# Retention attention and a hard-swish feed-forward layer: from whole sequences to 128-position chunks, with DMA transposes and a Strassen down product

## The chip, the cores and the metric

The kernel runs on one core of a Trainium2 chip. The metric is the device time of one execution in microseconds. A kernel is timed several times and beside runs of the kernel before on the same chip. A product is summed in PSUM, TensorE's output memory; an eviction reads it from there, computes on it and writes the result to SBUF, the memory that matmuls read. The span is the time from the first to the last instruction of a run. In the profiles PE is TensorE (matmul), PEld its weight loads, DVE is VectorE, ACT is ScalarE, POOL is GpSimd, and SP is the engine whose queue issues most DMAs.

## The reference, cut to what matters

```python
batch, n_heads, seq, head_dim = (8, 8, 576, 64)     # q, k, v: float32
scores = (1 / 8) * q @ k.T                          # per batch and head
gamma  = 1 - 2 ** (-5 - h)                          # one decay per head
ret    = scores * where(i >= j, gamma ** (i - j), 0)
x      = (ret @ v) -> [8 * 576, 512]                # heads side by side
h = x @ w_in                                        # 512 -> 2048
g = h * clip(h + 3, 0, 6) / 6
out = g @ w_out                                     # 2048 -> 512, float32
```

There is no softmax: the decay is a power of the distance. So the part of a row that lies in earlier chunks can be carried as a 64 x 64 state per head.

Of the kernel before, what the change touches and what calls it, by code (L numbers as in the profile page):

```python
# [10 lines left out]
FP32 = mybir.dt.float32  # L12
# [6 lines left out]
def kernel(  # L19
# [9 lines left out]
    nc = tc.nc  # L29
    B, H, S, D = q.shape  # L30
# [3 lines left out]

    NCH = (S + P - 1) // P
    msz = [min(P, S - P * i) for i in range(NCH)]
    m1sub = []
    for tcix in range(NCH):
        lo = P * tcix
        subs = []  # L40
        while lo < S:
            hi = min(lo + 512, S)
            subs.append((lo, hi))
            lo = hi
        m1sub.append(subs)
    atoff = []
    o = 0
    for tcix in range(NCH):
        atoff.append(o)
        o += S - P * tcix  # L50
    ATW = o
    m2sc = [(0, 288), (288, 576)]

    gamma = [1.0 - 2.0 ** (-5.0 - h) for h in range(H)]
    NFULL = S // P
    REM = S - NFULL * P

    const = ctx.enter_context(tc.tile_pool(name="const", bufs=1))
    work = ctx.enter_context(tc.tile_pool(name="work", bufs=3))
    big = ctx.enter_context(tc.tile_pool(name="big", bufs=1))  # L60

    ident16 = const.tile([P, P], FP16)
    make_identity(nc, ident16)
    cb = const.tile([P, 2], FP32)
    nc.gpsimd.memset(cb[:, 0:1], 0.5)
    nc.gpsimd.memset(cb[:, 1:2], float(np.log(0.125)))

    rsel = const.tile([P, ATW], FP32)
    for tcix in range(NCH):
        W = S - P * tcix  # L70
        nc.gpsimd.iota(rsel[:, atoff[tcix]:atoff[tcix] + W],
                       pattern=[[1, W]], base=0, channel_multiplier=-1,
                       allow_small_or_imprecise_dtypes=True)
        nc.gpsimd.affine_select(
            out=rsel[:, atoff[tcix]:atoff[tcix] + W],
            in_=rsel[:, atoff[tcix]:atoff[tcix] + W], compare_op=ALU.is_ge,
            fill=1.0e8, base=0, pattern=[[1, W]], channel_multiplier=-1)
    dmask = const.tile([P, H, ATW], FP16)
    for h in range(H):
        nc.scalar.activation(dmask[:, h, :], rsel, ACTF.Exp,  # L80
                             bias=cb[:, 1:2], scale=float(np.log(gamma[h])))

    win16 = big.tile([P, DM // P, DFF], FP16)
    wout16 = big.tile([P, DFF // P, DM], FP16)

    NCC = DM // P
    xt16 = big.tile([P, NCC, NTOK], FP16)

    psum = ctx.enter_context(tc.tile_pool(name="psum", bufs=8, space=bass.MemoryType.PSUM))

    def cast_load(src4, b, h, dst, coloff, width):
        last = (b == B - 1 and h == H - 1)
        if not last:
            fl = src4[b, h].rearrange("s d -> (s d)")
            ap = bass.AP(tensor=fl.tensor, offset=fl.offset,
                         ap=[[D, P], [P * D, NCH], [1, D]])
            nc.gpsimd.dma_start(dst[:, :, coloff:coloff + D], ap)
        else:
            nc.gpsimd.dma_start(
                dst[:, 0:NFULL, coloff:coloff + D],  # L100
                src4[b, h, 0:NFULL * P, :].rearrange("(j p) d -> p j d", p=P))
            nc.gpsimd.dma_start(dst[0:REM, NFULL, coloff:coloff + D],
                                src4[b, h, NFULL * P:S, :])
            nc.gpsimd.memset(dst[REM:P, NFULL, coloff:coloff + D], 0.0)

    NFC = DFF // P
    MBLK = 512
    NMB = NTOK // MBLK
    chunkq = []
    moe_state = {}  # L110

    def moe_unit(kb, kind, ix):
        tok0 = kb * MBLK
        if kind == 0:
            if ix == 0:
                moe_state[kb] = work.tile([P, NFC, MBLK], FP16, tag="gt16",
                                          bufs=2, name=f"gt16_{kb}")
            gt16 = moe_state[kb]
            fc = ix
            ph = psum.tile([P, MBLK], FP32, tag="pp")  # L120
            for dmc in range(NCC):
                nc.tensor.matmul(ph, win16[:, dmc, P * fc:P * fc + P],  # L122
                                 xt16[:, dmc, tok0:tok0 + MBLK],
                                 start=(dmc == 0), stop=(dmc == NCC - 1))
            u = work.tile([P, MBLK], FP32, tag="moeu", bufs=4)
            nc.scalar.activation(u, ph, ACTF.Relu, bias=cb[:, 0:1],  # L126
                                 scale=1.0 / 6.0)
            nc.vector.scalar_tensor_tensor(out=gt16[:, fc, :], in0=u,  # L128
                                           scalar=1.0, in1=ph,
                                           op0=ALU.min, op1=ALU.mult)  # L130
        else:
            gt16 = moe_state[kb]
            mc = ix
            pout = psum.tile([P, DM], FP32, tag="pp")
            for fc in range(NFC):
                nc.tensor.matmul(pout, gt16[:, fc, P * mc:P * mc + P],  # L136
                                 wout16[:, fc, :],
                                 start=(fc == 0), stop=(fc == NFC - 1))
            osb = work.tile([P, DM], FP32, tag="osb", bufs=4)
            nc.scalar.copy(osb, pout)  # L140
            nc.sync.dma_start(out[tok0 + P * mc:tok0 + P * mc + P, :], osb)

    def pop_units(n):
        for _ in range(n):
            if chunkq:
                moe_unit(*chunkq.pop(0))

    bready = [((kk + 1) * MBLK - 1) // S for kk in range(NMB)]
    xbar_i = [0]

    for b in range(B):
        if b > 0:
            for kk in range(NMB):
                if bready[kk] == b - 1:
                    for fc in range(NFC):
                        chunkq.append((kk, 0, fc))
                    for mc in range(MBLK // P):
                        chunkq.append((kk, 1, mc))
            pop_units(4)
        for c in range(H // 2):  # L160
            pop_units(1)
            qn16 = work.tile([P, NCH, 2 * D], FP16, tag="nat16", bufs=18)
            kn16 = work.tile([P, NCH, 2 * D], FP16, tag="nat16", bufs=18)
            vn16 = work.tile([P, NCH, 2 * D], FP16, tag="nat16", bufs=18)
            for h2 in range(2):
                cast_load(q, b, 2 * c + h2, qn16, h2 * D, D)
                cast_load(k, b, 2 * c + h2, kn16, h2 * D, D)
                cast_load(v, b, 2 * c + h2, vn16, h2 * D, D)
            qtk2 = []
            for nix, nat in enumerate((qn16, kn16)):  # L170
                pst = psum.tile([P, S], FP16, tag="pp")
                for j in range(NCH):
                    sj = msz[j]
                    nc.tensor.transpose(pst[:, P * j:P * j + sj],  # L174
                                        nat[0:sj, j, :], ident16[0:sj, 0:sj])
                sb = work.tile([P, S], FP16, tag="qtk", bufs=10)
                if nix == 0:
                    nc.vector.tensor_copy(sb, pst)  # L178
                else:
                    nc.scalar.copy(sb, pst)  # L180
                qtk2.append(sb)
            qt2, kt2 = qtk2
            pop_units(2)
            at16a = work.tile([P, ATW], FP16, tag="at16", bufs=6)
            at16b = work.tile([P, ATW], FP16, tag="at16", bufs=6)
            at16s = [at16a, at16b]
            bgrp = [[(0, 0, 512, 0)],
                    [(0, 512, S, 0), (1, P, S, 64)],
                    [(2, 2 * P, S, 0), (3, 3 * P, S, 320)],
                    [(4, 4 * P, S, 0)]]  # L190
            for grp in bgrp:
                pm0 = psum.tile([P, 512], FP32, tag="pp")
                pm1 = psum.tile([P, 512], FP32, tag="pp")
                pms = [pm0, pm1]
                for (tcix, a, bb, co) in grp:
                    mt = msz[tcix]
                    ns = bb - a
                    for h2 in range(2):
                        base = h2 * D
                        nc.tensor.matmul(pms[h2][0:mt, co:co + ns],  # L200
                                         kt2[base:base + D,
                                             P * tcix:P * tcix + mt],
                                         qt2[base:base + D, a:bb],
                                         start=True, stop=True)
# [11 lines left out]
            for (s0, s1) in m2sc:  # L216
# [4 lines left out]
                for tcix in range(NCH):  # L221
                    lo = max(s0, P * tcix)
                    if lo < s1:
                        contrib.append((tcix, lo))
# [32 lines left out]
    while chunkq:  # L257
        moe_unit(*chunkq.pop(0))
# [30 lines left out]
```

## The kernel before: what the change and the argument touch

All matmuls are fp16. For each batch and pair of heads it loads and casts q, k and v by DMA, transposes q and k on TensorE, computes all scores on and above the block diagonal (1600 columns per head), multiplies them by a stored decay table on VectorE, and multiplies by v. Units of the feed-forward product (up: 512-wide, down: 512-wide) are popped between these steps.

```python
for b in range(B):
    ...
    for c in range(H // 2):                          # a pair of heads
        pop_units(1)
        ...                                          # loads, 10 transposes, 2 copies
        pop_units(2)
        bgrp = [[(0, 0, 512, 0)], [(0, 512, S, 0), (1, P, S, 64)],
                [(2, 2 * P, S, 0), (3, 3 * P, S, 320)], [(4, 4 * P, S, 0)]]
        for grp in bgrp:
            ...                                      # scores into pm0, pm1 (PSUM)
            for h2 in range(2):
                nc.vector.tensor_tensor(             # the masked eviction
                    out=at16s[h2][0:mtg, alo:alo + wid],
                    in0=pms[h2][0:mtg, 0:wid],
                    in1=dmask[0:mtg, 2 * c + h2, alo:alo + wid], op=ALU.mult)
        pop_units(2)
        ...                                          # matmuls of v with at16s
        pop_units(1)
```

## Time and profile before

| | before |
|---|---|
| time, median of 2 | 455.52 us |
| span of the profiled run | 448.7 us |
| PE / DVE / ACT / POOL busy | 88 / 51 / 45 / 40% |
| first up product starts | 47.8 us |
| a batch in the middle | 48.4 us |

These are lines of the profile page of the kernel before: the span, the busy times, the busy tenths of PE and DVE in 40 slices, and the chain that ended last (from the last instruction back to what released it, and so on), by engine.

```profile
span 448.7 us, 6207 instructions
PE 394.0 (88%) x2368; PEld 181.7 (40%) x2368; DVE 230.5 (51%) x432; ACT 201.6 (45%) x349; POOL 177.6 (40%) x222
PE   0387999989998999899998999899989999899996
DVE  0254675347716672467635771667245763480540
PE 69%; DVE 18%; ACT 9%; issue 2%; POOL 1%; DVEq 0%; POOLq 0%
```

At first sight TensorE is full and VectorE half empty. But the chain gives VectorE 18%. The same kernel in order of time (start, duration, engine, line, output <- input) shows why. This is one pair of heads:

```profile
260.84 0.39 PE L200 MATMUL pm_2741<-sb 64*128 64x512 f16 x1
...
261.41 0.68 DVE L210 TENSOR_TENSOR at16a<-pm_2741,dmask 128x512 f16<-128x512 f32 x1
...
262.14 0.19 PE L200 MATMUL pm_2764<-sb 64*64 64x64 f16 x1 [0.33 <-DVE at16a L210]
262.60 0.69 DVE L210 TENSOR_TENSOR at16b<-pm_2742,dmask 128x512 f16<-128x512 f32 x1
262.74 1.89 PE L122 MATMUL ph<-xt_104,win_102 128*128 128x512 f16 x8 [0.41 <-DVE gt_4_2530 L128]
263.20 0.68 DVE L210 TENSOR_TENSOR at16a<-pm_2747,dmask 128x512 f16<-128x512 f32 x1
...
264.99 0.68 DVE L210 TENSOR_TENSOR at16b<-pm_2756,dmask 128x512 f16<-128x512 f32 x1
265.13 0.18 PE L230 MATMUL po_2785<-at16a,vn_2700 128*64 128x32 f16 x1 [0.19 <-DVE at16a L210]
```

All score matmuls but the last start within 0.8 us, but their six evictions of 128x512 follow one another every 0.6 us on VectorE, with one feed-forward operation (`gt`, 262.01, not shown) after the first. The brackets are TensorE's waits for VectorE, two for evictions and one for such a `gt`. The printed waits look small because a matmul's printed duration (379 ns for 512 columns) is longer than its share of the stream. The Trainium skill says so too ("Perfetto Trace Analysis", section "Identifying the Most-Contended Engine"): matmul busy share is no good measure of distance to the limit. The pace of the matmuls is seen in the chain at the end of the kernel, where nothing but feed-forward work is left (start, us, what):

```profile
403.41 13.81 PE pout L136 x64
417.23 13.81 PE ph L122 x64
```

Sixty-four matmuls take 13.8 us, 216 ns each. The feed-forward products, 1152 such matmuls, are thus 249 us of the 448.7. (The prediction calls them MoE products, after the names of the inputs.)

### The profile page before, as it was taken

The numbers are of one execution on the slowest core, as the hardware profiler recorded it, in microseconds if no ns is written. First come the engines' busy times: TensorE is split into PE (matmuls) and PEld (weight loads), VectorE is DVE, ScalarE is ACT, GpSimd is POOL, SyncE is SP. The second block draws the span as 40 slices with busy tenths as digits, with TensorE's granted clock in tenths as the row PEclk, the third lists the DMA queues.
The fourth block names the chain that finished last, engine by engine and source line by source line (L and its number), as shares of the span: only waits on it lengthen the run. The fifth ranks groups of instructions, "written<-read, shape, count | busy, mean of one in ns | idle before, by whom it ended". The sixth has DMA issues, their size and how long they took to land.

```text
span 448.7 us, 6207 instructions
## 1 busy us (share of the span) xinstructions
PE 394.0 (88%) x2368; PEld 181.7 (40%) x2368; DVE 230.5 (51%) x432; ACT 201.6 (45%) x349; POOL 177.6 (40%) x222
## 2 busy tenths in 40 slices
PE   0387999989998999899998999899989999899996
PEld 0133444434443444444443444344443444344442
DVE  0254675347716672467635771667245763480540
ACT  5623564156522663356415652266325641571641
POOL 9966799763534444155326353445200000000000
PEclk9999999999998999999999999999998999999999
DMA  5999999985777766487568568776210001001101
GB/s 36 123 189 192 120 96 96 154 75 37 46 92 88 46 45 61 86 55 50 37 101 74 39 44 93 87 50 42 39 70 1 0 1 70 26 0 48 47 23 70
DMA packets 134700, 29.73 MB, mean 66 GB/s; under 512 B 126480, under 2 KB 130064, under 8 KB 134672
## 3 DMA queue, kind: packets, MB, share of 16 engines
q0 software_dynamic: 129488, 19.91, 60.8%
q1 hardware_dynamic: 5184, 9.44, 5.7%
q8 instruction: 18, 0.29, 0.3%
q14 instruction: 10, 0.08, 0.1%
HBM read 39.80 MB, written 9.44 MB: 110 GB/s over the span
## 4 chain that ended last, share of the span: by engine, by line
PE 69%; DVE 18%; ACT 9%; issue 2%; POOL 1%; DVEq 0%; POOLq 0%
PE pout L136 28%; PE ph L122 22%; DVE at16a L210 8%; DVE at16b L210 6%; PE pst L174 5%; ACT dmask L80 3%; ACT xt_104 L236 2%; ACT u L126 2%; ACT sb L180 2%; DVE gt_6_3580 L128 1%; DVE gt_5_3055 L128 1%; DVE gt_0_430 L128 1%; DVE gt_4_2530 L128 1%; DVE gt_3_2005 L128 1%; DVE gt_2_1480 L128 1%
## 5 line engine op out<-in xcount | busy, mean ns | idle before, releaser
L122 PE MATMUL ph<-xt_104,win_102 128*128 128x512 f16 x576 | 143.2, 383 | 5.7 <-DVE gt_1_955 L128 0.8
L126 ACT ACTIVATE u<-ph,cb 128x512 f32<-128x512 f32 x144 | 97.2, 687 | 53.2 <-PE ph L122 51.0
L122 PEld LDWEIGHTS <-win_102 128*128 128x128 f16 x576 | 52.6, 97 | 71.0 <-issue 19.5
L140 ACT COPY osb<-pout 128x512 f32<-128x512 f32 x36 | 21.1, 585 | 111.5 <-PE pout L136 111.5
L178 DVE COPY sb<-pst 128x576 f16<-128x576 f16 x32 | 14.5, 455 | 43.3 <-PE pst L174 43.3
L200 PEld LDWEIGHTS <-sb 64*128 64x128 f16 (+1 forms) x384 | 14.9, 100 | 42.5 <-ACT sb L180 18.2
L180 ACT COPY sb<-pst 128x576 f16<-128x576 f16 x32 | 20.4, 637 | 3.6 <-PE pst L174 1.6
L128 DVE SCALAR_TENSOR_TENSOR gt_8_4320<-u,ph 128x512 f16<-128x512 f32 x16 | 11.0, 688 | 16.6 <-ACT u L126 16.6
L128 DVE SCALAR_TENSOR_TENSOR gt_6_3580<-u,ph 128x512 f16<-128x512 f32 x16 | 10.7, 681 | 9.0 <-ACT u L126 8.9
L128 DVE SCALAR_TENSOR_TENSOR gt_2_1480<-u,ph 128x512 f16<-128x512 f32 x16 | 10.5, 679 | 9.2 <-ACT u L126 9.2
L128 DVE SCALAR_TENSOR_TENSOR gt_5_3055<-u,ph 128x512 f16<-128x512 f32 x16 | 10.7, 681 | 8.0 <-ACT u L126 7.8
L128 DVE SCALAR_TENSOR_TENSOR gt_4_2530<-u,ph 128x512 f16<-128x512 f32 x16 | 10.7, 681 | 8.0 <-ACT u L126 7.8
L128 DVE SCALAR_TENSOR_TENSOR gt_0_430<-u,ph 128x512 f16<-128x512 f32 x16 | 10.5, 680 | 8.3 <-ACT u L126 8.3
L128 DVE SCALAR_TENSOR_TENSOR gt_1_955<-u,ph 128x512 f16<-128x512 f32 x16 | 10.5, 680 | 8.1 <-ACT u L126 8.1
L128 DVE SCALAR_TENSOR_TENSOR gt_3_2005<-u,ph 128x512 f16<-128x512 f32 x16 | 10.5, 680 | 8.1 <-ACT u L126 8.1
L136 PE MATMUL pout<-wout_103,gt_2_1480 128*128 128x512 f16 x64 | 14.3, 379 | 0.2 <-DVE at16a L210 0.2
L136 PE MATMUL pout<-wout_103,gt_4_2530 128*128 128x512 f16 x64 | 14.3, 379 | 0.2 <-DVE at16a L210 0.2
L136 PE MATMUL pout<-wout_103,gt_0_430 128*128 128x512 f16 x64 | 14.3, 379 | 0.2 <-DVE at16a L210 0.2
L136 PE MATMUL pout<-wout_103,gt_1_955 128*128 128x512 f16 x64 | 14.3, 379 | 0.2 <-DVE at16a L210 0.2
L136 PE MATMUL pout<-wout_103,gt_5_3055 128*128 128x512 f16 x64 | 14.3, 379 | 0.2 <-DVE at16a L210 0.2
L136 PE MATMUL pout<-wout_103,gt_6_3580 128*128 128x512 f16 x64 | 14.3, 379 | 0.2 <-DVE at16a L210 0.2
L136 PE MATMUL pout<-wout_103,gt_3_2005 128*128 128x512 f16 x64 | 14.3, 379 | 0.2 <-DVE at16a L210 0.2
(1059 smaller groups left out, 775.9 us busy)
## 6 DMA issues: line engine op xcount, KB each, us to landing
out_dram<-osb SPq DMA_DIRECT2D x36, 256.0 KB, 2.0
win_102<-in_moe_w_in_dram POOLq DMA_DIRECT2D x2, 640.0 KB, 8.8
wout_103<-in_moe_w_out_dram POOLq DMA_DIRECT2D x2, 640.0 KB, 10.0
win_102<-in_moe_w_in_dram POOLq DMA_DIRECT2D x1, 768.0 KB, 9.9
wout_103<-in_moe_w_out_dram POOLq DMA_DIRECT2D x1, 768.0 KB, 10.5
qn_108<-in_q_dram POOLq DMA_DIRECT2D x2, 80.0 KB, 3.0
kn_109<-in_k_dram POOLq DMA_DIRECT2D x2, 80.0 KB, 3.0
vn_110<-in_v_dram POOLq DMA_DIRECT2D x2, 80.0 KB, 3.1
```

The source lines that it names most:

```text
L80: nc.scalar.activation(dmask[:, h, :], rsel, ACTF.Exp, bias=cb[:, 1:2], scale=float(np.log(gamma[h])))
L122: nc.tensor.matmul(ph, win16[:, dmc, P * fc:P * fc + P], xt16[:, dmc, tok0:tok0 + MBLK], start=(dmc == 0), stop=(dmc == NCC - 1))
L126: nc.scalar.activation(u, ph, ACTF.Relu, bias=cb[:, 0:1], scale=1.0 / 6.0)
L128: nc.vector.scalar_tensor_tensor(out=gt16[:, fc, :], in0=u, scalar=1.0, in1=ph, op0=ALU.min, op1=ALU.mult)
L136: nc.tensor.matmul(pout, gt16[:, fc, P * mc:P * mc + P], wout16[:, fc, :], start=(fc == 0), stop=(fc == NFC - 1))
L140: nc.scalar.copy(osb, pout)
L174: nc.tensor.transpose(pst[:, P * j:P * j + sj], nat[0:sj, j, :], ident16[0:sj, 0:sj])
L178: nc.vector.tensor_copy(sb, pst)
L180: nc.scalar.copy(sb, pst)
L200: nc.tensor.matmul(pms[h2][0:mt, co:co + ns], kt2[base:base + D, P * tcix:P * tcix + mt], qt2[base:base + D, a:bb], start=True, stop=True)
L210: nc.vector.tensor_tensor(out=at16s[h2][0:mtg, alo:alo + wid], in0=pms[h2][0:mtg, 0:wid], in1=dmask[0:mtg, 2 * c + h2, alo:alo + wid], op= ...
L236: nc.scalar.copy(xt16[h2 * D:h2 * D + D, c, b * S + s0:b * S + s1], pos[h2][h2 * D:h2 * D + D, 0:s1 - s0])
```

## The change

Its intent: do attention in linear time, transposes by DMA, and one eighth less of the down product.

- A unit is 128 positions of one batch, all heads (36 units; the last 4 hold the 64-position tails of two batches). Units take the batches in turn. The decay inside a chunk is folded into q and v by per-position scales, so the score mask is only 0 or 1. The past is a state `X` per batch.
- q is written zero-padded, one 128-row slot per head, so that scores and state products contract over 128 rows.
- From unit 8 on, q and k are transposed by DMA, issued from SP.
- The down product of a block of 512 tokens uses Strassen's scheme, which multiplies 2 x 2 blocks with 7 block products instead of 8 at the price of sums of blocks: products of 256 columns, the sums mostly on VectorE, running sums in PSUM, of which ScalarE copies the states that are needed later (snapshots).
- The order is written out by hand in slots: one sixteenth of a block's `up` (4 matmuls) and one half-product of `down` (8 matmuls) per slot, a unit's attention every 4 slots. The first `down` is at slot 24 (`DSTART`).

```diff
-        for grp in bgrp:                      # all blocks of the sequence
-            ...
+    def sc(u, hf):                            # scores: diagonal block only
+        ...
+            for h0 in (0, 64):
+                mm(ps[h0:h0 + 64, i], kT[u][:, pr, h0:h0 + 64], qT[u][:, pr], i == 0, True)
+        ...                                   # one masked eviction of 128x512 on VectorE
+    def pu(u):                                # k^T v, added to the state, decayed on POOL
+        ...
+    def ou(u):                                # v with at[u], plus X with qT[u]
+        ...
-            for fc in range(NFC):
-                nc.tensor.matmul(pout, gt16[:, fc, P * mc:P * mc + P], wout16[:, fc, :], ...)
+    PROD = ["M1", "M2", "M4", "M6", "M5", "M7", "M3"]
+    def down(n, hp):                          # half of one Strassen product
+        ...
+        for j in range(8):
+            mm2(ps[:, mt], a[:, j, P * mt:P * mt + P], w[:, j, :], ...)   # 256 columns
+    ...
+    for u in range(4, NU):
+        tu = 16 * (u // 4 - 1) + 4 * (u % 4)
+        at_t(tu, lambda u=u: (sc(u, 0), sc(u, 1)), 2)
+        at_t(tu + 2, lambda u=u: pu(u), 2)
+        at_t(tu + 2, lambda u=u: ou(u), 2)
+        at_t(tu - 6 if u >= 8 else tu - 1, lambda u=u: (tr if u >= 8 else trpe)(u))
+        at_t(tu - 9, lambda u=u: cast(u, POOL, POOL, POOL))
+        if u >= 7:
+            at_t(tu - 9 - LEAD, lambda u=u: load(u))
+    ...                                       # up in every slot, down from slot 24
```

## The prediction

> **What bounds it now.** TensorE. The page has PE busy 394 of 448.7 us (88%), DVE 51%, ACT 45%, POOL 40%; the chain that ended last is 69% PE. The two MoE products are 576 matmuls of 512 columns each. In the chain in order of time, 64 such matmuls take 13.8 us at the end, 216 ns each, so the products are 2 x 124.4 = 249 us. The rest, about 200 us, is attention (about 48.4 us per batch in the timeline, of which about 31 are MoE, so 17 us of attention and its waits, 138 us in all) and a start of 50 us before the first up product.
>
> **What the change does.**
> 1. Down product: Strassen with 7 of 8 block products, 9 x 14 x 8 = 1008 matmuls of 256 columns instead of 576 of 512. The Trainium skill ("TensorE: Matmul & The Clock Gate", "Wait — 56ns, not 53.3ns?") gives N / 2.4 GHz + 2.5 ns start to start; the trace agrees at 512 (216 ns). So 109 ns each (estimate): 110 us instead of 124, if weight loads stay hidden. The 128-column transposes start every 85-90 ns in the timeline, so loads need less than 109. Saves 14 us.
> 2. Attention: linear in sequence (128-position chunks with a running state), no decay table of 1600 columns, no score evictions beyond the diagonal. I estimate 1.5-2.1 us of PE per unit including about 0.1 us for each switch between half-width and full-width matmuls (seen in the timeline around score and value matmuls), times 36: 54-75 us instead of 138. Saves 60-80 us.
> 3. Start: eight 1.6-us mask activations and the descriptor writing on POOL (about 0.9 us per load issue) go; loads move to the SP queue. First up product at about 25-30 us instead of 50.
> 4. Added: 36 casts on POOL, estimated 4-5 us per unit from the 2.6 cycles per element of "GPSIMD Engine Reference", "Elementwise — side-by-side cycle accounting" (no run shows it yet); DMA transposes for 28 units; 72 Strassen sums of about 0.6 us on DVE; snapshots of about 0.6 us on ACT (the 128x512 eviction takes 585 ns). Per 16 slots I get DVE 24, ACT 16, POOL 20 us against PE about 34: off the critical path.
>
> **Sum.** Start 27 us; 24 slots before the first down product, about 35 us of PE but probably 45, as loads of 256-byte rows plus 8 MB of weights (about 18 MB by then) limit it; 120 slots of up and down 104 + 99 us plus 30 units, 60 us; last Strassen block 12.5 us; last store 4; total about 345-350, plus the 6.8 us by which the time exceeds the span. Predicted 350 us, range 322 to 388. Faster by over 2%: 0.95; within 2%: 0.02; slower: 0.03.
>
> **What would show it.** 1: 1008 down matmuls starting every 109-112 ns. 2: attention's share of PE under 2.1 us per unit. 3: first up product before 32 us. 4: DVE under 80%, POOL under 65% busy in the middle; PE over 90% busy from 80 us on, ending the chain. Waits of DVE or PE on DMA transposes should be absent there.
>
> **What would make it wrong.** Rows of 256 bytes through the SP queue slower than 150 GB/s (then DMA bounds the first 100 us or all); DMA transposes taking over 8 us per unit, or delaying the loads behind them in the one SP queue; POOL casts over 8 us per unit, or locking with DVE's two-input sums; half-width matmuls not running in pairs (adds up to 40 us); PE waiting on single-buffered down accumulators (estimated 0.5 us per block).

## More of the kernel before

The runs of the kernel before spread from 449 to 457 us, most of them at 449 to 452 or at 454 to 457 us, on every chip used; why was not looked into. (Three of them, at 456.8 to 457.2 us, are marked slow and left out of the ratios.) The profiled run of the kernel before is one of the quicker ones: other runs with about its span took 450 to 452 us.

## The result, and the profile after

The new kernel took 354.18 us (353.17 to 355.18, 2 runs) against 455.52 us (454.57 to 456.48, 2 runs). The ratio is 0.781, 95% interval 0.766 to 0.796. Ratios here are the mean time of one kernel's fast runs over that of the other's of the same rounds, so not quite the ratio of the medians quoted.

The lines of the page of the new kernel that answer to those above, with the granted TensorE clock and the DMA share per slice added:

```profile
span 353.4 us, 7092 instructions
PE 307.5 (87%) x2768; PEld 195.1 (55%) x2768; DVE 239.1 (68%) x392; ACT 153.0 (43%) x235; POOL 162.1 (46%) x228
PE   3653568977989999999999999999999999999882
DVE  4671464769965984895797599569649955954810
PEclk9975886989999999999999999999999999999998
DMA  9989999999997499899479989948998500200305
PE 70%; DMA 11%; DVE 9%; SPq 4%; issue 2%; ACT 1%; POOL 0%; DVEq 0%; POOLq 0%
```

TensorE's busy share is the same, but its gaps now lie in the first quarter, where DMA is at 9. Cut at the first down product (88.5 us) and at the last block's (330.7 us), the windows read as follows (window: length, then busy us and instructions of PE, PEld, DVE, ACT and POOL, granted clock, DMA share, which can print above 1 and is used here only for comparison, GB/s):

```profile
0.00:88.50 88.50, 56.21 (x461) 29.31 (x461) 51.38 (x99) 35.14 (x54) 47.20 (x86) 0.85 1.12 217
88.50:330.70 242.20, 238.46 (x2198) 154.99 (x2197) 180.55 (x283) 114.76 (x176) 113.62 (x142) 1.00 0.74 143
330.70:353.40 22.70, 12.87 (x113) 10.78 (x111) 7.14 (x12) 3.11 (x6) 1.27 (x1) 0.93 0.26 70
```

In the middle TensorE streams nearly without a gap. From the timeline of PE there:

```profile
165.17 1.03 PE L53 MATMUL up<-xt,win 128*128 128x512 f16 x4
166.13 0.63 PE L53 MATMUL sc<-qT,kT 128*64 128x256 f16 x8
166.69 1.05 PE L53 MATMUL accD2M<-tw,su 128*128 128x256 f16 x8
167.57 1.03 PE L53 MATMUL up<-xt,win 128*128 128x512 f16 x4
```

Starts matter here, not durations. Four up matmuls take 4 x 216 ns, 0.86 us (165.17 to about 166.03), 8 down matmuls 0.88 us (166.69 to 167.57), so 109 ns for 256 columns. The scores of a unit take 0.66 us (from about 166.03 to 166.69); the rest of the unit takes 0.78 us in the same listing. A unit is 1.44 us, so a batch (4.5 units) 6.5 us of TensorE. Before, a batch in the middle held 128 feed-forward matmuls (64 up, 64 down), 27.6 us, so its attention and the waits were 48.4 - 27.6 = 20.8 us. (The prediction counted about 31 us of feed-forward work per batch; two whole blocks are left for the end.)

The first 88.5 us are the expensive part. They hold 24 slots of up (20.8 us), 10 units (14.4 us) and the 8 units transposed on TensorE (8 x 0.7 us), 41 us of work at full speed. For the other 47 us or so TensorE waited or ran at a lower granted clock: that was 0.85 over this window and 0.62 from 20 to 30 us, and the first four up matmuls took 1.84 us instead of 0.86. The SP queue shows the loads held up from 15 us on (start, us the issue took):

```profile
15.17 0.54 SPq L162 DMA_DIRECT2D stgq<-in_q_dram  x1
15.76 5.30 SPq L162 DMA_DIRECT2D stgk<-in_k_dram  x1
21.10 4.38 SPq L162 DMA_DIRECT2D stgv<-in_v_dram  x1
```

An issue that took about 0.5 us at first (0.82 us into the run) takes 4 to 5 us there. What holds it was not tested.

### The profile page after: what moved, and what is told of

The parts are those of the page before. It is cut to its first block, busy times and chain, and to the rows that moved or that the text cites. A ratio compares the mean times of both kernels' runs of the same rounds, so it can differ in the third digit from the quotient of the medians.

```text
span 353.4 us, 7092 instructions
## 1 busy us (share of the span) xinstructions
PE 307.5 (87%) x2768; PEld 195.1 (55%) x2768; DVE 239.1 (68%) x392; ACT 153.0 (43%) x235; POOL 162.1 (46%) x228
## 4 chain that ended last, share of the span: by engine, by line
PE 70%; DMA 11%; DVE 9%; SPq 4%; issue 2%; ACT 1%; POOL 0%; DVEq 0%; POOLq 0%
PE up L53 30%; DMA stgk<-in_k_dram 7%; PE sc L53 4%; SPq L162 3%; PE O L53 3%; DMA wstg<-in_moe_w_in_dram 3%; DVE gt L283 2%; DVE su L295 2%; PE accA4M L53 2%; PE accA3M L53 2%; PE accA2M L53 2%; PE accA5M L53 2%; PE accA6M L53 2%; PE accA1M L53 2%; PE accA8M L53 2%
## 5 line engine op out<-in xcount | busy, mean ns | idle before, releaser
L282 ACT ACTIVATE u<-up,cb 128x512 f32<-128x512 f32 x144 | 99.1, 688 | 138.9 <-PE up L53 132.1
L53 PE MATMUL up<-xt,win 128*128 128x512 f16 x576 | 150.6, 390 | 1.2 <-DVE gt L283 1.2
L283 DVE SCALAR_TENSOR_TENSOR gt<-u,up 128x512 f16<-128x512 f32 x144 | 98.3, 684 | 71.2 <-ACT u L282 70.6
L53 PEld LDWEIGHTS <-win 128*128 128x128 f16 x576 | 56.5, 100 | 46.9 <-issue 8.5
L53 PEld LDWEIGHTS <-su 128*128 128x128 f16 x576 | 54.2, 98 | 19.8 <-issue 5.2
L53 PEld LDWEIGHTS <-gt 128*128 128x128 f16 x432 | 40.7, 98 | 18.2 <-issue 7.0
L220 DVE TENSOR_TENSOR at<-sc,maskc 128x512 f16<-128x512 f32 x64 | 41.0, 681 | 5.4 <-PE sc L53 5.4
L184 POOL TENSOR_TENSOR v<-stgv,gv 128x512 f16<-128x512 f32 x36 | 38.4, 1066 | 8.2 <-DMA stgv<-in_v_dram 8.1
L182 POOL TENSOR_TENSOR qpad<-stgq,gq 128x256 f16<-128x256 f32 x64 | 40.4, 651 | 0.0
L295 DVE TENSOR_TENSOR su<-gt 128x1024 f16<-128x1024 f16 x36 | 30.2, 840 | 0.0
L53 PEld LDWEIGHTS <-kT 128*64 128x64 f16 x288 | 14.4, 116 | 20.8 <-issue 15.0
L205 PEld LDWEIGHTS <-qpad 128*128 128x128 f16 x64 | 5.5, 125 | 27.4 <-POOL qpad L182 15.9
```

Of the source, the lines that this page charges most:

```text
L53: nc.tensor.matmul(o, l, r, start=start, stop=stop, skip_group_check=True)
L182: eq.tensor_tensor(out=qp[:, :, a, 64 * a:64 * a + 64], in0=s[:, :, a, :], in1=bc(ga), op=ALU.mult)
L184: ev.tensor_tensor(out=v16[u], in0=stg["v", u], in1=bc(gv), op=ALU.mult)
L205: nc.tensor.transpose(ps[:, i], src[:, i], ident)
L220: nc.vector.tensor_tensor(out=at[u][:, 2 * hf:2 * hf + 2].rearrange("p c a s -> p (c a) s"), in0=ps.rearrange("p c a s -> p (c a) s"), in1 ...
L282: nc.scalar.activation(ut, ph, ACTF.Relu, bias=cb[:, 0:1], scale=1.0 / 6.0)
```

## The experiments

My theory after the first look had four parts: (1) the gain comes mainly from VectorE's evictions, for which TensorE had waited, not from TensorE's own work; (2) in the middle TensorE is the limit, so Strassen and the DMA transposes are worth their matmul time; (3) the start is limited by loads in rows of 256 bytes; (4) changes between half-width and full-width matmuls cost TensorE about 0.1 us each. The rivals are in the expectations. Unless said otherwise an experiment edits the new kernel, was timed in 3 rounds (4 runs), and gave correct results.

Differences of a few us need care. Four chips took part in the experiments (e1 to e4, e5 to e8, e9 to e11, and e12), and the new kernel itself was timed only in its own 2 runs. In the runs that load in the same order (the new kernel, e1, e6, e7, e8, e10) the scores of unit 8, at slot 16, start at 73.3, 70.7, 71.3, 70.1, 70.8 and 70.8 us: the new kernel's only profile is the latest, though none of these edits changes the loads before it. So where an experiment gains about 5 us, 2 to 3 us of it may be this start and not the edit. The stretch from these scores to the first down product of the last block leaves the start out; it is 257.5 us in the new kernel.

### e1: the ordinary down product instead of Strassen's

```diff
-    DSTART = 24
+    DSTART = 16
-    def down(n, hp):          # Strassen
+    def down(n, hp):          # ordinary: a quarter of one 128-token product
+        mc, qt = divmod(hp, 4)
+        ...
+        for fc in range(4 * qt, 4 * qt + 4):
+            mm2(ps, gt[n][:, fc, P * mc:P * mc + P], wout16[:, fc, :], fc == 0, fc == NFC - 1)
+        ...                    # one copy on ScalarE, then the store; no sums, no snapshots
```

> The new kernel with the ordinary down product (64 matmuls of 512 columns a block) in place of Strassen's (112 of 256), first down product at slot 16 of the schedule instead of 24. Theory A (TensorE bounds the steady part, Strassen is worth its matmul time): 9 blocks x (13.8 - 12.2) = 14 us more of TensorE, less 3 to 8 us because VectorE loses the sums that fill it between 75 and 100 us and the start is earlier: 360 to 366 us. Rival B (the sums, snapshots and half-size matmuls cost as much as Strassen saves): 356 us or less.

Measured: 354.1 us (353.43 to 355.39), as long as the new kernel and in rival B's range. But neither expectation separates Strassen from the earlier start, because two things were changed at once (the ordinary product holds its operand longer and needs the earlier start). Run e5 takes them apart.

### e2: all transposes on TensorE

```diff
-        at_t(tu - 6 if u >= 8 else tu - 1, lambda u=u: (tr if u >= 8 else trpe)(u))
+        at_t(tu - 1, lambda u=u: trpe(u))
```

> The new kernel with all 36 units transposed on TensorE (before: the first 8) and no DMA transposes. Theory A (TensorE-bound): 28 units x 12 transposes x 85 ns = 28 us more, 376 to 384 us. Rival B (the DMA transposes slow the loads and hold up the SP queue, so moving them away gives back 10 us or more): under 370 us.

Measured: 367.8 us, 13.6 us more. That is in the rival's range, but only part of the reason is the rival's. The trace shows the 12 transposes of a unit in 0.67 us (up product again at 219.53 after the transposes began at 218.86), 56 ns each and not the 85 ns that I had read from the kernel before. So 28 units cost 28 x 0.7 = 19 us, not 28. Of these, 2.8 us came back before slot 24 (first down product at 85.7 us), no more than the start differs between runs anyway. The DMA transposes are worth about 14 us net, half of what I had expected.

### e3: the kernel before with short evictions (wrong values on purpose)

```diff
-                        out=at16s[h2][0:mtg, alo:alo + wid],
-                        in0=pms[h2][0:mtg, 0:wid],
-                        in1=dmask[0:mtg, 2 * c + h2, alo:alo + wid],
+                        out=at16s[h2][0:mtg, alo:alo + 64],
+                        in0=pms[h2][0:mtg, 0:64],
+                        in1=dmask[0:mtg, 2 * c + h2, alo:alo + 64],
```

(The six buffers of `at16s` are allocated once and cleared at the start, so that nothing unwritten is read.)

> The kernel before with every masked score eviction cut to its first 64 columns (result wrong on purpose), TensorE's instructions unchanged. Theory A (attention before was long because TensorE waited for VectorE's 0.68-us evictions, and the new kernel gains by having only 72 of them): 390 to 412 us. Rival B (its attention was long by TensorE's own work, which the linear form cuts): 440 us or more.

Measured: 392.1 us (391.92 to 393.15) against 454.5 us on the same chip; values wrong as intended. The page of this run, busy times and the chain by engine:

```profile
span 390.1 us, 6352 instructions
PE 350.8 (90%) x2368; PEld 168.8 (43%) x2368; DVE 150.0 (38%) x438; ACT 200.8 (51%) x349; POOL 177.5 (46%) x222
PE 81%; DMA 7%; POOL 5%; ACT 5%; issue 1%; DVE 0%; DVEq 0%; POOLq 0%
```

VectorE has left the chain (18% before), and the kernel, with the same 2368 matmuls, takes 62 us less (59 by the spans of the two profiles). The chain gives the period of a batch. First the kernel before, then this run:

```profile
73.41 3.45 PE pout L136 x16
...
121.77 3.45 PE pout L136 x16
```

```profile
65.20 3.45 PE pout L139 x16
...
106.14 3.45 PE pout L139 x16
```

So 48.4 us became 40.9 us per batch. Attention's share, less the 27.6 us of feed-forward matmuls, fell from 20.8 to 13.3 us without one matmul less. The linear form with its 1.44 us per unit (6.5 us per batch) takes away another 6.8 us per batch. Theory A holds for its number: about half of what attention gave in a batch was waiting for evictions, and about 60 us of the 101 us of the whole gain. The other half is mostly TensorE's own work, as rival B has it: in a batch of this run TensorE is busy for 39.8 of the 40.9 us. VectorE was only 51% busy over the whole run, but within a pair of heads it was the limit.

### e4: loads in long rows (wrong values on purpose)

```diff
-                eng.dma_start(t[p0:p0 + nr], src[b, :, P * c:P * c + nr, :]
-                              .rearrange("h s d -> s h d"))
+                eng.dma_start(t[p0:p0 + nr], src[b].rearrange("h s d -> (h s d)")
+                              .rearrange("(s h d) -> s h d", h=H, d=D)[P * c:P * c + nr])
```

> The new kernel reading the same number of bytes of q, k and v in rows of 2 KB instead of 256 bytes (wrong values on purpose). Theory A (the first 70 us wait for loads that 256-byte rows slow down): the loads land sooner, the first down product moves from 88 to about 70 us and the total falls to 332 to 345 us. Rival B (the start is bound by bytes, by the issue in the SP queue, or by POOL's casts): 350 us or more.

Measured: 341.4 us, 12.8 us less. The first two windows of this run, then of the new kernel (columns as above; the last is GB/s):

```profile
0.00:20.00 20.00, 10.18 (x92) 6.57 (x92) 11.44 (x35) 6.88 (x12) 10.35 (x35) 1.00 0.93 330
20.00:40.00 20.00, 12.21 (x113) 7.31 (x114) 8.43 (x16) 6.97 (x11) 14.44 (x20) 1.00 1.10 327
```

```profile
0.00:20.00 20.00, 10.18 (x92) 6.56 (x92) 11.23 (x35) 6.88 (x12) 10.30 (x35) 1.00 1.15 227
20.00:40.00 20.00, 10.20 (x100) 5.86 (x100) 9.18 (x16) 6.77 (x10) 9.26 (x13) 0.66 1.00 216
```

With the same number of issues in the same queue, 330 GB/s arrive instead of 227. The first down product moved from 88.5 to 75.1 us, and the whole gain lies there. So neither the number of issues nor POOL's casts set the pace of the start, but the short rows. (The granted clock was higher too, 1.00 instead of 0.66 from 20 to 40 us; no run separates what this gave from what the faster loads gave.) The Trainium skill says that rows this short cost DMA throughput ("DMA: Bandwidth & Descriptors", section "Why small descriptors are slow (HBM only)"); its example for 256 bytes has 27% overhead, the case shows 330 / 227, 45% more with long rows.

### e5: Strassen kept, down product from slot 16

```diff
-    DSTART = 24
+    DSTART = 16
```

> The new kernel, Strassen kept, with the first down product at slot 16 instead of 24 (and so the weight sums at slots 8 to 15 instead of 16 to 23). The run with the plain product at slot 16 took 354.1 us, as long as Strassen at slot 24. Theory A (that run gained about 14 us from the earlier down product, which fills TensorE's idle time before 100 us, and lost 14 us by the plain product): 338 to 346 us. Rival B (the earlier start brings nothing, and Strassen's matmul saving is eaten by its sums and snapshots): 351 us or more.

Measured: 348.7 us, between the two. Against e1, which differs in the down product alone (with its sums, accumulators and stores), Strassen is worth 354.1 - 348.7 = 5.4 us (the runs are on two chips; the fast runs of the kernel before have medians of 454.5 and 452.4 us there), although it saves 9 x 1.6 = 14 us of matmuls. The traces show where it went. From slot 16 to the last block Strassen takes 251.6 us (73.0 to 324.6) against 260.9 us (71.3 to 332.2), 9.3 us less. It reaches slot 16 1.7 us later, with VectorE busy for 18.9 us of the 20 us from 60 us on, weight sums among it (10.0 us in e1). And from the start of the last block to the end it takes 22.7 us against 19.5 us: its 12.2 us of matmuls wait twice 1.4 us for a sum on VectorE that reads a single-buffered accumulator, and its last stores come in one burst.

### e6: only the weight sums earlier

```diff
-        at_t(DSTART - 8 + 2 * i, lambda i=i: wsum(i, 0, 4, DVE), 4)
-        at_t(DSTART - 7 + 2 * i, lambda i=i: wsum(i, 4, 8, DVE), 4)
+        at_t(DSTART - 16 + 2 * i, lambda i=i: wsum(i, 0, 4, DVE), 4)
+        at_t(DSTART - 15 + 2 * i, lambda i=i: wsum(i, 4, 8, DVE), 4)
```

> The new kernel with only the 8 weight sums moved 8 slots earlier (slots 8 to 15); down product still from slot 24. Theory A (VectorE, busy 20.0 of the 20 us from 80 to 100 us, holds TensorE up there): 346 to 351 us. Rival B (the loads decide when slot 24 is reached, VectorE only fills the wait): 353 us or more.

Measured: 349.4 us, 4.8 us less, as theory A said. The window of the new kernel that made me suspect it, and the same window of e6:

```profile
80.00:100.00 20.00, 15.89 (x146) 9.37 (x143) 20.00 (x31) 7.92 (x12) 12.68 (x16) 1.00 1.06 189
```

```profile
80.00:100.00 20.00, 18.70 (x188) 11.71 (x186) 17.17 (x27) 9.72 (x16) 12.47 (x16) 1.00 1.11 198
```

VectorE is busy for all of the 20 us. With the sums earlier it was 17.2 us and TensorE went from 15.9 to 18.7 us. From the scores of unit 8 to the last block e6 takes 254.2 us, 3.3 us less than the new kernel; this much is the edit's, and the rest is the earlier start. So behind the loads a second limit had stood, which the averages (68% over the span) do not show.

### e7 and e8: what changes of matmul width cost

e7 computes the scores full-width; e8 turns on the kernel's own switch that makes the up and down products pairs of half-width matmuls.

```diff
-            for h0 in (0, 64):                                   # e7
-                mm(ps[h0:h0 + 64, i], kT[u][:, pr, h0:h0 + 64], qT[u][:, pr],
-                   i == 0, True)
+            mm(ps[:, i], kT[u][:, pr, :], qT[u][:, pr], i == 0, True)
```

```diff
-    PAIR = False                                                 # e8
+    PAIR = True
```

> The new kernel with the scores as 4 full-width matmuls per unit instead of 8 half-width ones, all else the same. Theory A (each change between half-width and full-width costs TensorE about 0.1 us; the score group takes 0.66 us for 4 x 0.109 us of streaming): 36 x 0.2 us less, 345 to 349 us. Rival B (no cost of the change: the 0.66 us is something else, such as the weight loads): 353 us or more.

> The new kernel with its own switch PAIR on: up and down products as pairs of half-width matmuls too, so that nothing switches width after the first 8 units. Theory A (half-width pairs stream as fast as one full-width matmul, 0.109 us per 256 columns as seen in the score groups, and the 4 width changes per unit cost 0.45 us): 36 x 0.45 = 16 us less, 335 to 343 us. Rival B (half-width weight loads are not hidden behind 256 columns or the doubled count of instructions binds): 358 us or more.

Measured: e7 349.2 us, 5.0 us less, just outside its theory A. Its score group takes 0.44 us in the trace instead of 0.66, as the theory says, but from the scores of unit 8 to the last block it takes 252.8 us, 4.7 us less, where 28 x 0.22 = 6.2 us were due. e8 347.6 us, 6.6 us less: faster, but less than theory A's 16 us. The mechanism is plain in e8's timeline:

```profile
161.18 1.06 PE L53 MATMUL up<-xt,win 128*64 128x512 f16 x8
162.05 0.63 PE L53 MATMUL sc<-qT,kT 128*64 128x256 f16 x8
162.48 1.07 PE L53 MATMUL accD2M<-tw,su 128*64 128x256 f16 x16
163.36 1.06 PE L53 MATMUL up<-xt,win 128*64 128x512 f16 x8
```

The same 8 score matmuls take 0.43 us instead of 0.66 us, the second half of a unit 0.57 us instead of 0.78 us, and the pairs of up and down stream as before (0.87 and 0.88 us). So a unit gains 0.44 us, a change of width costs about 0.11 us. The Trainium skill names the cause without a number ("TensorEngine Tiling (Array Packing)", section "Key Properties"): changing the tiling mode drains TensorE. The estimate of 16 us was wrong in the count. The 10 units before slot 24 gain nothing, since TensorE waits there anyway, and 26 x 0.44 = 11 us remain. Of these, the stretch from slot 24 to the last block shows 5.7 us (236.5 us instead of 242.2 us). TensorE's listed waits from 100 us to the last block rose by 2.5 us (2.1 to 4.6 us), mostly for the one sum that frees the accumulator of the second product, so part of the gain became a new wait. The other 3 us or so I have not traced.

### e9: only the order of the first loads

```diff
         load_win(i, nc.sync)
-        if i:
-            load(3 + i)
+        if i < 3:
+            load(4 + i)
...
-    cast_win(1, (ACT, DVE))
-    for i in range(4):
-        load_wout(i)
...
+    at_t(2, lambda: cast_win(1, (ACT, DVE)))
+    for i in range(4):
+        at_t(2 * i, lambda i=i: load_wout(i))
```

> The new kernel with only the order of the first loads changed: unit 4 right after the first quarter of the up weights, 5 and 6 one step earlier too, and the four loads of the down weights issued during slots 0 to 6 instead of before slot 0. The bytes are the same. Theory A (TensorE's waits of 6.6, 4.0 and 3.4 us before units 4, 5 and 6 come from their loads standing behind weights that are needed later): 346 to 351 us. Rival B (all of it is needed soon and the bytes decide; the wait only moves to later units): 353 us or more.

Measured: 354.1 us, no gain. The total fits rival B, yet the trace does not: the waits before units 4, 5 and 6 shrank from 6.6, 4.0 and 3.4 us to 3.1, 0 and 0, and one new wait swallowed all of it. In the timeline of PE, then of the SP queue:

```profile
71.47 1.06 PE L53 MATMUL sc<-qT,kT 128*64 128x256 f16 x8 [14.18 <-DMA kT<-k]
```

```profile
59.60 3.89 SPq L162 DMA_DIRECT2D stgv<-in_v_dram  x1
...
66.47 2.37 SPq L189 DMA_TRANSPOSE qT<-qpad  x1
68.93 1.21 SPq L192 DMA_TRANSPOSE kT<-k  x1
```

TensorE stood for 14.2 us before unit 8, the first one transposed by DMA. Its casts on POOL had ended at 56.1 us, but its transposes stand in the same queue behind loads, of which two are held up for 4 to 5 us each, and were issued at 66.5 us. Had I believed the time alone, I would have called the bytes the limit.

### e10, e11, e12: a version that beats both

e10 joins the parts: pairs everywhere, first down product at slot 16, the ordinary product for the first and last block (where Strassen's sums and waits had cost more than they saved), weight sums at slots 16 to 23, last stores from two queues. e11 adds e9's order of loads. e12 adds TensorE transposes for units 8 to 11.

```diff
-    DSTART = 24
-    PAIR = False
+    DSTART = 16
+    PAIR = True
...
+        PL = n in (0, NB - 1)
-        for hp in range(14):
-            at_t(d + hp, lambda n=n, hp=hp: down(n, hp), 3)
+        for hp in range(16 if PL else 14):
+            at_t(d + hp, lambda n=n, hp=hp, f=plain if PL else down: f(n, hp), 3)
...
-        at_t(tu - 6 if u >= 8 else tu - 1, lambda u=u: (tr if u >= 8 else trpe)(u))      # e12
+        at_t(tu - 6 if u >= 12 else tu - 1, lambda u=u: (tr if u >= 12 else trpe)(u))
```

> A version meant to be faster than both kernels: half-width pairs everywhere, first down product at slot 16, ordinary product for the first and the last block and Strassen for the seven between, the weight sums at slots 16 to 23 where nothing waits for them, and the last stores issued from two queues. From the parts: slot 16 at about 71 us as with the plain product, 16 slots plain 31.7 us, 7 blocks of about 30.5 us, last block and end 18 us: 334 to 340 us. If the gains of the early down product and of the pairs (5.5 and 6.6 us) come from the same idle time they don't add: 343 us or more.

> The mix with the changed order of first loads. If that order is worth what theory A of the order run says: 3 to 8 us less than the mix. If bytes decide: within 1.5 us of the mix.

> The mix with the changed order of loads, and units 8 to 11 transposed on TensorE too, DMA transposes from unit 12 on. In both runs with the changed order TensorE's waits before units 4 to 6 shrank, but one wait of 14 us for the first DMA transpose (unit 8) stood in their place. Theory A (that transpose stood behind the loads in the one SP queue; four units' transposes on TensorE cost 4 x 0.7 us and let the gain of the order through): 326 to 333 us. Rival B (the bytes decide when the work of slots 16 to 24 can be done, whoever transposes): 336 us or more, against 338.6 and 337.9 us of the two mixes.

Measured: e10 337.9 us, e11 338.6 us, e12 327.8 us (327.06 to 328.64), 0.725 of the kernel before (interval 0.720 to 0.730). e11 repeated e9's result with a wait of 14.5 us for unit 8's transposes. e12 took that wait away and took 10.8 us less than e11 (on another chip), 10.1 less than e10. Its windows:

```profile
40.00:60.00 20.00, 17.02 (x212) 11.27 (x209) 15.58 (x27) 13.28 (x21) 12.66 (x18) 1.00 1.09 197
60.00:80.00 20.00, 20.00 (x244) 11.77 (x240) 17.97 (x28) 9.69 (x16) 17.55 (x22) 1.00 1.12 225
```

TensorE is full from 60 to 80 us, with the first down product, at slot 16, at 60.1 us instead of 73.4 us in e11 and 71.3 us in e10. The mix with TensorE transposes for units 8 to 11 but the old order of loads was not run, so the order's share is not shown apart; in e2, with the old order, transposes on TensorE brought slot 24 only 2.8 us forward. So rival B of e9 and e12 falls: in the start two things stood in line, the short rows (e4) and the one queue in which transposes wait behind loads (e9 against e12).

## Why the prediction was right or wrong

The time, 354.2 us, lies within the range and near the 350 us named. It is right in its sum, but partly because errors cancel. By the cuts of the trace:

| term | predicted | measured |
|---|---|---|
| start and 24 slots | 27 + 45 = 72 us | 88.5 us |
| 120 slots of up and down, with units | 104 + 99 + 60 = 263 us | 242.2 us |
| last block and last store | 12.5 + 4 = 16.5 us | 22.7 us |
| time over span | 6.8 us | 1.8 us (355.18 us for a span of 353.4 us) |

The parts as written add up to 351.5 us and not to "about 345-350", and with 6.8 us to 358 us; I rounded towards 350 without a reason.

1. Down product. "1008 down matmuls starting every 109-112 ns" is right: 109 ns. The rule that it took from the Trainium skill ("TensorE: Matmul & The Clock Gate", section "Wait — 56ns, not 53.3ns?"; 216 ns at 512 columns and, worked out from it, 109 ns at 256) agrees with the trace at both sizes. "Saves 14 us" is right for TensorE's work, wrong for the time: e5 against e1 gives 5.4 us, the rest lost at start and end and in short waits.
2. Attention. The size 1.5-2.1 us per unit was a little high (1.44 us), and the share of width changes, 0.1 us each, was right (0.11 us). I multiplied by 30 units where 26 lie after slot 24. "138 us of attention and its waits" rests on about 31 us of feed-forward work per batch, where the trace has 27.6, and on eight batches, where the start of 50 us already holds the first; the errors nearly cancel (7 x 20.8 = 146 us). The 32 units after the new start take 32 x 1.44 = 46 us, so attention gave about 100 us against the predicted 60-80, and the waits of the first 88.5 us took some of it back. What the prediction didn't see is why: e3 shows that about 60 us of the old time was waiting for evictions on an engine that it had listed as 51% busy. It counted "no score evictions beyond the diagonal" as one item among several.
3. Start. "First up product at about 25-30 us" came at 33.4 us, past the 32 us of its own test. The mis-sized term is what follows: I allowed 45 us for 24 slots, and they took 55. The warning in "what would make it wrong", that transposes delay or stand behind the loads in the one SP queue, holds (2.8 us listed in the new kernel, 14 us in e9). So does that of the 256-byte rows, if not below the 150 GB/s named: 217 GB/s was already too little.
4. Side engines. DVE under 80% and POOL under 65% in the middle hold (180.6 and 113.6 of 242.2 us, 75 and 47%). POOL's v cast took 1066 ns for 512 elements per partition; the 2.6 cycles per element of the Trainium skill ("GPSIMD Engine Reference", section "Elementwise — side-by-side cycle accounting") give 1.1 us, an estimate at the 1.2 GHz that the section uses, so the rate fits. The 4-5 us per unit were too much: the casts of a full unit took 704 + 2 x 651 + 1066 ns, 3.1 us. "PE over 90% busy from 80 us on" failed for 20 us: VectorE was the limit from 80 to 100 us (e6, about 3 us), a stretch hidden in its average. "Off the critical path" was said for the mean of 16 slots and did not look at the slots in which weight sums, block sums and evictions meet.
5. Single-buffered accumulators: estimated 0.5 us per block; 0.2 to 0.5 us in the middle, but 1.1 us in the first block and 2.8 us in the last, where no other work fills the wait.
6. The time over the span: 6.8 us compared one profile with the median of other runs. The kernel before has runs near 450 us as well as near 456 us, and the profile was of a quick one; a profile must be compared with its own run's time.

What stays open: where some 3 of the 11 us that e8 should gain after slot 24 went; why the start of the new kernel differs by 2 to 3 us between runs, and whether the chip has a part in it; what the spread of the kernel before is; what the order of loads is worth without the other parts of e12; and how much of the start is due to short rows once the queue is free (no long-row version of e12 was run).

## What to carry to other kernels

Ask of each stage which wait ends last, not which engine is busiest on average: a half-busy VectorE cost about 60 us before and about 3 us after, both times in a burst. A time that doesn't move is no proof that a change did nothing: read where the gain went, since here one new 14-us wait for a transpose behind loads in the same queue hid most of a gain of about 10 us. Where an algorithm saves matmuls with extra sums, use it where other work covers the sums; at the start and the end it cost more than it saved here (e5 against e1), though leaving it out there was only tried together with other changes (e10).

## What the Trainium skill lacked or had wrong

- "TensorE: Matmul & The Clock Gate", "Part 4: PE-mode transpose", gives about 275 to 390 ns for a 128x128 transpose. Streamed between other matmuls, 12 of them took 0.67 us here (e2), 56 ns start to start, while the printed duration of one was 219 ns; so the page's figure is no measure of what one more transpose in a stream costs.
- "TensorEngine Tiling (Array Packing)", "Key Properties", says that a change of tiling mode drains TensorE but not for how long: about 0.11 us per change here (0.44 us for the four of a unit). Its list of restrictions says that column tiling turns off the fast weight load; 16 half-width matmuls of 256 columns, each with its own weights, took 0.88 us, as long as 8 full-width ones, so no loss is seen at this size.
- "DMA: Bandwidth & Descriptors" does not say how long a DMA transpose of these sizes holds the issuing queue, nor that the issue of a load can be held up: in the SP queue of the new kernel a transpose took 2.0 us for 128x1024 (median; 1.2 to 3.5) and 1.3 us for 128x512 (1.2 to 2.2), and the issue of one 256-KB load of 256-byte rows up to 5.3 us. No page that I read warns that a DMA transpose then waits behind loads (14 us).
